# Narrowing one of eight weight groups in a later stage of a fused attention and mixer kernel

## The chip, the cores and the metric

The kernel runs on one core of one Trainium2 chip. The metric is device time in microseconds (us) of one execution, the median of several runs. Engines are named as in the profile: PE is TensorE (matmuls; PEld is its weight load), DVE is VectorE, ACT is ScalarE, POOL is GpSimd, SP is SyncE, whose queue issues all the DMAs spoken of here.

## What is computed

Three blocks follow each other on 8 sequences of 576 tokens with 512 features. The change touches a weight of the third.

```python
# 1 attention in chunks of 64 tokens, 8 heads of 64
# 2 h = relu(x @ w_in); conv over 3 tokens; (h * sigmoid(conv)) @ w_out
# 3
X = fft(fft(x, axis=1), axis=2)
u = x + real(X)
un = (u - mean(u)) / sqrt(var(u) + 1e-6)
out = u + relu(un @ w_ch1) @ w_ch2        # w_ch1 512 x 2048, w_ch2 2048 x 512
```

Weights arrive as 64-bit floats and are narrowed to 32 bits by the kernel itself.

## The kernel before

**Stages.** In the first part the kernel runs attention, block 2 and the Fourier transforms, half a sequence (16 of them) at a time. In the second part it computes relu(un @ w_ch1) in six chunks of tokens and, in each chunk, eight groups g = 0 to 7 of features (`group`, six-matmul products on L855). The third part multiplies by w_ch2 (`second`, L922). Each of the last two products is a block scheme with seven products in place of eight: each group has the products B11, B21, T2, T1, T3, T4 and B22, and their weights are four blocks of w_ch1 and four sums of blocks, T1 to T4.

**Weights of the second part.** For each group of w_ch1, `weight_sums` loads two pieces of 512 KB (`wide`), narrows each with `to_float32` (four DVE instructions, L278, L279, L281 and L282, and one ACT instruction, L280), makes the four sums in `block_sums` (DVE, one on L661 and three on L660), and stores blocks and sums to the DRAM scratch `t_scr` (L668 for the blocks, L669 for the sums). This happens in the first part for all eight groups, one started every 9 steps. For w_ch2 the same work, `weight_sums_late`, runs within chunks 1 to 4 of the second part.

**From the scratch back.** `load_tw(0, g)` brings a group back in two pieces, k = 0 (512 KB: the weights of B11, B21, T2, T1) and k = 1 (384 KB: T3, T4, B22), each into a staging tile `ts`, and splits it into `th` (ACT cast, L265) and `tl` (DVE subtraction, L266). A product multiplies th by sxh, th by sxl and tl by sxh, in this order, so its third matmul needs `tl`. The split tiles of groups 0 to 7 stay for all chunks; chunk 0 is where they are filled. The tiles of groups 2 to 7 lie in a pool `e` that takes the room of pools of the first part, and so wait for the last users of that room.

**The ring of ts.** `ts` has three buffers, used strictly in the order in which the program asks for them: a tile starts when the third tile before it is done with (all writers and readers). `weight_sums_late` takes three tiles of this ring at once: `wide` (also the place of the sums), `x` and `both`.

```python
            ring = plan.rings.setdefault((pool, tag), [])
            self.before = ring[-bufs] if len(ring) >= bufs else None
        wide, x, both = (buf("b", "ts", 3, *shape) for shape in (([128, 512], I64), ([128, 512],), ([128, 1024],)))
```

**What sets the order.** A planner (`Plan.emit`) simulates the engines with a cost for each operation and writes out a fixed order for each engine's queue: of the operations that are ready by its own clock, the one with the lowest priority number goes first. A priority unit is about 1 us in the second part, where group g of chunk 0 has priorities from `start + 7 * g`. On the chip each queue runs in that order and waits at each operation for what it needs.

**Order of ts in chunk 0.** The tiles are asked for in this order: group 0 (two), one for the left operands, group 1 (two), group 2 (two), group 3 (two), and so on to group 7.

Of the kernel before, what the change touches and what calls it, by code (L numbers as in the profile page):

```python
# [8 lines left out]
F32 = mybir.dt.float32  # L9
# [11 lines left out]
FT = 8  # L21
# [15 lines left out]
FG = 8  # L37
# [48 lines left out]
class Plan:  # L86
# [10 lines left out]
    def buf(self, pool, tag, bufs, shape, dtype=F32):  # L97
        return Buf(self, pool, tag, bufs, shape, dtype)

    def op(self, eng, cost, fn, prio, r=(), w=(), after=(), nbytes=0, spare=0):  # L100
        o = Op()
        o.spare = spare
        o.eng, o.cost, o.fn, o.prio, o.nbytes, o.seq = eng, cost, fn, prio, nbytes, len(self.ops)
        o.slots = [b for b in w if b.tag in self.ANY_ORDER and not b.writers]
        deps = {}
        for b in r:
            assert b.writers and not b.closed, b.tag
            for d in b.writers:
                deps[d] = True
        for b in w:  # L110
            assert not b.closed, b.tag
            if not b.writers:
                if b.pool in self.opened:
                    deps[self.opened[b.pool]] = True
                if b.before is not None:
                    for d in b.before.writers + b.before.readers:
                        deps[d] = True
                if b.previous is not None and b.previous not in w:
                    deps.setdefault(b.previous.writers[0], False)
            for d in b.writers + b.readers:  # L120
                deps[d] = True
        for d in after:
            deps[d] = True
        for b in r:
            b.readers.append(o)
        for b in w:
            b.writers.append(o)
        o.held = [b for b in {id(b): b for b in (*r, *w)}.values() if b.tag in self.ANY_ORDER]
        for b in o.held:
            b.left += 1  # L130
        o.deps, o.users = deps, []
        for d in deps:
            d.users.append(o)
        o.left, o.ready, o.end = len(deps), 0.0, None
        self.ops.append(o)
        return o
# [73 lines left out]
def kernel(  # L210
# [44 lines left out]
    def load(dst, src, nbytes, prio, r=(), after=()):  # L255
        return op("SP", 450, lambda: sp.dma_start(out=dst(), in_=src()), prio, r=r, w=[dst], after=after, nbytes=nbytes)

    def vop(n, fn, prio, r, w, fast=False, scalars=0):
        return op("DVE", dve_cost(n, fast, scalars), fn, prio, r=r, w=w)
# [13 lines left out]
    def to_float32(f, x, wide, n, prio, view=lambda t: t):  # L273

        word = lambda t, k: t.rearrange("p (n two) -> p n two", two=2)[:, :, k]
        lo, hi = lambda: word(wide().bitcast(U32), 0), lambda: word(wide().bitcast(U32), 1)
        ff, fb, xb = lambda: view(f()), lambda: view(f()).bitcast(U32), lambda: x().bitcast(U32)
        vop(n, lambda: dve.tensor_scalar(xb(), hi(), 3, 0x3FFFFFF8, op0=ALU.logical_shift_left, op1=ALU.bitwise_and), prio, [wide], [x], fast=True)  # L278
        vop(n, lambda: dve.scalar_tensor_tensor(fb(), in0=hi(), scalar=0xC0000000, in1=xb(), op0=ALU.bitwise_and, op1=ALU.bitwise_or), prio, [wide, x], [f])  # L279
        aop(n, lambda: act.activation(out=x(), in_=word(wide().bitcast(F32), 1), func=ACT.Abs), prio, [wide], [x])  # L280
        vop(n, lambda: dve.scalar_tensor_tensor(fb(), in0=lo(), scalar=29, in1=fb(), op0=ALU.logical_shift_right, op1=ALU.bitwise_or), prio, [wide, f], [f])  # L281
        vop(n, lambda: dve.scalar_tensor_tensor(ff(), in0=x(), scalar=LEAST_NORMAL, in1=ff(), op0=ALU.is_ge, op1=ALU.mult), prio, [x, f], [f])  # L282
# [371 lines left out]
    def block_sums(n, g, a, b, r, ts, tv, prio):  # L654

        lo, hi = slice(0, 256), slice(256, 512)
        b11, b12, b21, b22 = ((a, lo), (b, lo), (a, hi), (b, hi)) if n == 0 else ((a, lo), (a, hi), (b, lo), (b, hi))
        at = lambda x: x[0]()[:, x[1]]
        t = lambda i: tv()[:, 256 * (i - 2):256 * (i - 2) + 256]
        sub = lambda i, x, y: vop(256, lambda: dve.tensor_tensor(t(i), x(), y(), op=ALU.subtract), prio, [*r, ts], [ts])  # L660
        vop(256, lambda: dve.tensor_tensor(t(T1), at(b12), at(b11), op=ALU.subtract), prio, r, [ts])  # L661
        sub(T2, lambda: at(b22), lambda: t(T1))
        sub(T3, lambda: at(b22), lambda: at(b12))
        sub(T4, lambda: at(b21), lambda: t(T2))
        dst = t_scr[n][g]
        parts = [(0, 512, a, slice(0, 512))] if n == 0 else [(0, 256, a, lo), (256, 512, b, lo)]
        for c0, c1, x, xs in [*parts, (1536, 1792, b, hi)]:
            op("SP", 450, lambda c0=c0, c1=c1, x=x, xs=xs: sp.dma_start(out=dst()[:, c0:c1], in_=x()[:, xs]), prio + 0.5, r=r, w=[dst], nbytes=512 * (c1 - c0))  # L668
        op("SP", 450, lambda: sp.dma_start(out=dst()[:, 512:1536], in_=tv()), prio + 0.5, r=[ts], w=[dst], nbytes=524288)  # L669
# [10 lines left out]
        ts = buf("w", "wide", 2, [128, 1024])  # L680
        block_sums(0, g, *fs, fs, ts, ts, prio + 3.5)

    def weight_sums_late(g, srcs, prio):

        wide, x, both = (buf("b", "ts", 3, *shape) for shape in (([128, 512], I64), ([128, 512],), ([128, 1024],)))
        for k, src in enumerate(srcs):
            load(wide, lambda src=src: src, 524288, prio - 8 + 2 * k)
            to_float32(both, x, wide, 512, prio + 2 * k, view=lambda t, k=k: t[:, 512 * k:512 * k + 512])
        a, b = (lambda k=k: both()[:, 512 * k:512 * k + 512] for k in range(2))
        block_sums(1, g, a, b, [both], wide, lambda: wide().bitcast(F32), prio + 4)  # L690

# [8 lines left out]
    def load_tw(n, g, prios):  # L702
        tw[n, g] = []
        for k, (c0, c1) in enumerate(CUTS):
            s = buf("b", "ts", 3, [128, c1 - c0])
            src = t_scr[n][g]
            op("SP", 450, lambda s=s, src=src, c0=c0, c1=c1: sp.dma_start(out=s(), in_=src()[:, c0:c1]), prios[k] - 6, r=[src], w=[s], nbytes=512 * (c1 - c0))
            hl = tuple(buf("b" if g < 2 else "e", f"t{x}{k}{g}", 1, [128, c1 - c0], F32R) for x in "hl")
            tw[n, g].append(hl)
            if (n, g) == (0, 0):  # L710
                whole["t", k] = s
            split(*hl, s, c1 - c0, prios[k], after=() if n or g else last_fold)
# [240 lines left out]
        load_weight(w_in[:, f, :], wi, -2 + f)  # L953
        load_weight(w_out[:, f, :], wo, 0 + f)
    rows = lambda src: [[src[:, f, :] for f in (g, FG + g)] for g in range(FG)]
    later = list(enumerate(rows(w_ch1)))
    for i in range(NH):
        t = i * FT
        if i + 1 < NH:
            for q in range(2):  # L960
                attention(i + 1, q, t - 3.5 + 3 * q)
        for f in range(FT):
            step = m_step(i, f, t + f)
            x_step(i, f, t + f + lag)
            while later and t + f >= FT + 9 * (FG - len(later)):
                weight_sums(*later.pop(0), t + f + 8, [step])
            if t + f == 88:
                stats_first([88 + 2 * n for n in range(2 * HT)])
            if t + f in (103, 111, 119):
                norm_first((t + f - 103) // 8, t + f)  # L970
        if i == 0:
            load_dft(14)
        if i % 2:
            b, t = i // 2, t + FT + lag
            fold(b, t + 1)
            for sine in range(2):
                for m in range(3):
                    d_step(b, m, sine, t + 2.5 + m + 0.5 * sine)
            for m in range(3):
                s_step(b, m, t + 5 + m if b == B - 1 else t + 6 + 2 * m)  # L980
# [17 lines left out]
    start = end + 8  # L998
# [3 lines left out]
    begun = [group(0, 0, end)]  # L1002
    for g in range(1, FG):
        load_tw(0, g, [start + 7 * g - 7, start + 7 * g - 3])
    for c in range(NCH):
        t = start + span * c
        begun = begun if c == 0 else []
        for g in range(len(begun), FG):
            begun.append(group(c, g, t + 7 * g))
            if 1 <= c <= 4 and g in (0, 2):  # L1010
                n = 2 * (c - 1) + g // 2
                weight_sums_late(n, rows(w_ch2)[n], t + 7 * g + 10)
        if c + 1 < NCH:
            prep(c + 1, [t + 7 * g for g in (2, 3, 4, 4, 5, 6)], [begun[g] for g in ((1, 3) if c else (3, 5))])
    t = start + span * NCH
# [125 lines left out]
```

## Time and profile before

| | us |
|---|---|
| median of 3 runs (1356.93 to 1362.35) | 1359.32 |
| the profiled execution | 1358.73 |
| its span, first to last instruction | 1357.0 |
| PE busy in the span | 1322.6 (97%) |
| DVE busy | 1048.2 (77%) |
| ACT busy | 801.2 (59%) |

The page gives busy time per engine over the span. PE's matmuls follow each other at a fixed pace when nothing holds them: 42 matmuls of 384 columns of one group take about 7.3 us. The granted clock is 0.996 of full speed on average.

### The profile page before, as it was taken

Reading aid. Unit: us, or ns where it says so; the run is one execution under the profiler, and the core shown is the slowest. Engines: PE = TensorE matmul, PEld = TensorE weight load, DVE = VectorE, ACT = ScalarE, POOL = GpSimd, SP = SyncE. Lnnn points to the kernel's source line nnn. Section 1 sums busy time; section 2 is a strip of 40 time slices with the busy share of each in tenths; the row PEclk is TensorE's granted clock in tenths of the full one; section 3 lists DMA queues with packets and bytes.
Section 4 is the critical chain, followed back from the end, with each engine's and each line's share of the span. In section 5 each row is a group of like instructions: output and inputs, shape, how many; then the busy total and the mean of one; then the engine's idle time right before and its main releaser. Section 6 shows DMA issues by size and latency. Waiting matters only on the chain.

```text
span 1357.0 us, 29644 instructions
## 1 busy us (share of the span) xinstructions
PE 1322.6 (97%) x11362; PEld 1288.9 (95%) x11362; DVE 1048.2 (77%) x2017; ACT 801.2 (59%) x2181; POOL 73.4 (5%) x190
## 2 busy tenths in 40 slices
PE   5899999999999999998999999999999999999999
PEld 4699999999999999987999999999999999999998
DVE  7999897889977676767777676765598777777773
ACT  6777675868676676646766665656763333333331
POOL 1111020101001110200000000000000000000000
PEclk9999999999999999998999999999999999999999
DMA  8523614232522132135766657669855554554441
GB/s 307 159 84 116 191 58 151 83 123 95 187 87 79 62 116 60 57 128 175 250 189 186 201 163 230 183 194 294 247 160 182 174 173 133 164 171 142 154 140 40
DMA packets 154573, 206.50 MB, mean 152 GB/s; under 512 B 11584, under 2 KB 103360, under 8 KB 154432
## 3 DMA queue, kind: packets, MB, share of 16 engines
q1 hardware_dynamic: 154432, 204.61, 48.1%
q8 instruction: 89, 1.46, 0.4%
q14 instruction: 52, 0.43, 0.1%
HBM read 130.51 MB, written 74.06 MB: 151 GB/s over the span
## 4 chain that ended last, share of the span: by engine, by line
PE 91%; DVE 4%; ACT 2%; issue 1%; DMA 0%; POOL 0%; ACTq 0%; DVEq 0%
PE x L855 21%; PE x L922 15%; PE o L451 14%; PE x L516 14%; PE o L922 11%; PE o L855 4%; PE o L586 3%; PE o L614 2%; PE o L635 1%; PE o L371 1%; PE o L748 1%; PE o L414 1%; PE o L396 1%; DVE cv L468 0%; DMA h_scr<-u 0%
## 5 line engine op out<-in xcount | busy, mean ns | idle before, releaser
L265 ACT CAST sxh<-raw 128x1024 fp32r<-128x1024 f32 (+1 forms) x149 | 146.6, 990 | 186.6 <-PE x L922 83.7
L451 PE MATMUL o<-x,wih 128*128 128x320 f32 (+1 forms) x960 | 198.8, 301 | 1.6 <-DVE x L428 1.0
L266 DVE TENSOR_TENSOR sxl<-raw,sxh 128x1024 fp32r<-128x1024 f32 (+1 forms) x149 | 170.0, 1150 | 35.8 <-ACT sxh L265 35.5
L855 PE MATMUL x<-sxh,th 128*128 128x384 f32 x564 | 190.2, 337 | 2.7 <-ACT th L265 2.1
L855 PE MATMUL x<-sxh,tl 128*128 128x384 f32 x564 | 189.3, 336 | 0.8 <-DVE tl L266 0.8
L855 PE MATMUL x<-sxl,th 128*128 128x384 f32 x564 | 188.8, 335 | 0.0
L922 PE MATMUL x<-th,sxl 128*128 128x256 f32 x576 | 163.3, 283 | 0.5 <-DVE sxl L266 0.5
L922 PE MATMUL x<-th,sxh 128*128 128x256 f32 x576 | 163.3, 283 | 0.2 <-ACT h L832 0.2
L922 PE MATMUL x<-tl,sxh 128*128 128x256 f32 x576 | 163.2, 283 | 0.0
L451 PEld LDWEIGHTS o<-x,wih 128*128 128x128 f32 x960 | 153.3, 188 | 3.9 <-DVE x L428 1.4
L468 DVE SCALAR_TENSOR_TENSOR cv<-h,cw,cv 128x255 f32<-128x255 f32 (+2 forms) x256 | 129.2, 515 | 30.7 <-ACT cv L482 22.8
L823 DVE TENSOR_TENSOR u<-x,u 128x384 f32<-128x384 f32 (+1 forms) x168 | 83.5, 498 | 83.8 <-PE x L922 29.1
L516 PE MATMUL x<-gh,woh 128*128 128x322 f32 (+1 forms) x480 | 145.9, 304 | 0.5 <-ACT gh L265 0.5
L516 PE MATMUL x<-gl,woh 128*128 128x322 f32 (+1 forms) x480 | 142.4, 297 | 0.2
L516 PE MATMUL x<-gh,wol 128*128 128x322 f32 (+1 forms) x480 | 142.5, 297 | 0.0
L451 PE MATMUL o<-x,wil 128*128 128x320 f32 (+1 forms) x480 | 142.1, 296 | 0.0
L922 PE MATMUL o<-th,sxl 128*128 128x256 f32 x432 | 122.4, 283 | 0.0
L922 PE MATMUL o<-tl,sxh 128*128 128x256 f32 x432 | 122.4, 283 | 0.0
L922 PE MATMUL o<-th,sxh 128*128 128x256 f32 x432 | 122.4, 283 | 0.0
L922 PEld LDWEIGHTS x<-th,sxl 128*128 128x128 f32 x576 | 110.7, 192 | 0.7 <-DVE sxl L266 0.7
L922 PEld LDWEIGHTS x<-th,sxh 128*128 128x128 f32 x576 | 110.7, 192 | 0.5 <-ACT h L832 0.5
L922 PEld LDWEIGHTS x<-tl,sxh 128*128 128x128 f32 x576 | 110.7, 192 | 0.0
(273 smaller groups left out, 3217.8 us busy)
## 6 DMA issues: line engine op xcount, KB each, us to landing
raw<-h_scr SPq DMA_DIRECT2D x72, 512.0 KB, 4.4
h_scr<-u SPq DMA_DIRECT2D x96, 192.0 KB, 2.8
u<-u_scr SPq DMA_DIRECT2D x66, 256.0 KB, 4.3
qk<-in_qk_b SPq DMA_DIRECT2D x32, 320.0 KB, 3.5
h_scr<-m SPq DMA_DIRECT2D x48, 192.0 KB, 3.1
h_scr<-h SPq DMA_DIRECT2D x48, 192.0 KB, 2.8
out_y<-u SPq DMA_DIRECT2D x35, 256.0 KB, 2.4
wide<-in_w_ch SPq DMA_DIRECT2D x16, 512.0 KB, 4.3
```

The lines of the kernel that those rows point to most:

```text
L265: aop(n, lambda: act.copy(out=cut(h()), in_=cut(src())), prio, [src], [h], psum, after=after)
L266: vop(n, lambda: dve.tensor_tensor(cut(l()), cut(src()), cut(h()).bitcast(F32), op=ALU.subtract), prio, [src, h], [l])
L371: pe.matmul(s[h]()[half[u], slot, :], t[half[h], 0, ks], t[half[h], 1, ks], start=True, stop=True)
L396: pe.transpose(tps[k // 4]()[:, k % 4, :], flat[:, 128 * k:128 * k + 128], ident)
L451: pe.matmul(acc(), w[:, ws], x, start=k == 0, stop=k == 11)
L468: vop(hi - lo, lambda: dve.scalar_tensor_tensor(cv()[:, lo:hi], in0=h()[:, src:src + hi - lo], scalar=tap(k), in1=cv()[:, lo:hi], op0=ALU. ...
L516: pe.matmul(accs[d](), w[:, dsl], x, start=f == 0 and k == 0, stop=f == FT - 1 and k == 2)
L586: pe.matmul(acc()[:rows, :], x, w, start=n == 0, stop=n == len(todo) - 1)
L614: pe.matmul(accs[sine]()[:rows, :], w, x, start=n == 0, stop=n == len(todo) - 1)
L823: vop(n, lambda: dve.tensor_tensor(cut(x()), acc(), cut(x()), op=ALU.add), prio, [acc, x], [x])
L855: pe.matmul(acc(), a, b, start=first and m == 0, stop=m == 5, skip_group_check=not first)
L922: pe.matmul(acc(), a, b, start=first and m == 0 and gs[0] == 0, stop=gs[-1] == FG - 1 and m == len(todo) - 1, skip_group_check=not first)
```

## The change

The list `later` of the first part loses group 7 of w_ch1, and the remaining seven groups start every 10 steps and not every 9. The narrowing and summing of group 7 is done by `weight_sums_late`, which now takes the number of the weight as `m`. It is asked for in the loop that asks for the `load_tw` of chunk 0, right after that of group 2 and ahead of that of group 3, with priority `start + 10`.

```diff
-    def weight_sums_late(g, srcs, prio):
+    def weight_sums_late(g, srcs, prio, m=1):
...
-        block_sums(1, g, a, b, [both], wide, lambda: wide().bitcast(F32), prio + 4)
+        block_sums(m, g, a, b, [both], wide, lambda: wide().bitcast(F32), prio + 4)
...
-    later = list(enumerate(rows(w_ch1)))
+    later = list(enumerate(rows(w_ch1)[:FG - 1]))
...
-            while later and t + f >= FT + 9 * (FG - len(later)):
+            while later and t + f >= FT + 10 * (FG - 1 - len(later)):
                 weight_sums(*later.pop(0), t + f + 8, [step])
...
     for g in range(1, FG):
         load_tw(0, g, [start + 7 * g - 7, start + 7 * g - 3])
+        if g == 2:
+            weight_sums_late(FG - 1, rows(w_ch1)[FG - 1], start + 10, 0)
```

## Rows read from the trace of the kernel before

**Rows 1.** The page: busy time of each engine, share of the span, instructions.

```profile
PE 1322.6 (97%) x11362; PEld 1288.9 (95%) x11362; DVE 1048.2 (77%) x2017; ACT 801.2 (59%) x2181; POOL 73.4 (5%) x190
```

**Rows 2.** Busy time by stretch: length; PE, PEld, DVE, ACT, POOL busy; clock, DMA share, GB/s.

```profile
108.00:370.00 262.00, 259.88 (x2826) 251.04 (x2826) 230.17 (x548) 186.91 (x692) 32.35 (x88) 1.00 0.39 125
...
646.30:660.00 13.70, 13.70 (x81) 13.70 (x80) 10.84 (x22) 10.61 (x20) 0.00 (x0) 1.00 0.92 304
660.00:680.00 20.00, 20.00 (x125) 19.90 (x124) 16.57 (x36) 14.61 (x32) 0.00 (x0) 1.00 0.73 224
...
760.00:996.00 236.00, 235.85 (x1400) 234.94 (x1399) 157.12 (x297) 146.62 (x305) 0.00 (x0) 1.00 0.71 214
996.00:1357.00 361.00, 357.20 (x2975) 356.93 (x2974) 273.32 (x319) 128.29 (x125) 0.00 (x0) 1.00 0.47 148
```

**Rows 3.** Groups by line, 100 to 370 us: busy us, mean ns of one, idle before.

```profile
L282 DVE SCALAR_TENSOR_TENSOR wf<-wx,wf 128x512 f32<-128x512 f32 x15 | 10.3, 686 | 0.3
L660 DVE TENSOR_TENSOR wide<-wf,wide 128x256 f32<-128x256 f32 x16 | 6.7, 419 | 0.1
L278 DVE TENSOR_SCALAR wx<-wide 128x512 uint32<-128x512 uint32 x15 | 6.3, 419 | 0.1
```

**Rows 4.** SP's queue by time: start, us, DMA issues.

```profile
624.47 2.40 SPq L707 DMA_DIRECT2D ts<-t_scr  x3
630.96 0.57 SPq L707 DMA_DIRECT2D ts<-t_scr  x1
639.78 4.12 SPq L707 DMA_DIRECT2D ts<-t_scr  x3
...
677.30 5.73 SPq L880 DMA_DIRECT2D h_scr<-u  x2
```

**Rows 5.** DVE by time, the splits of groups 1 to 3 and one addition.

```profile
629.24 0.96 DVE L266 TENSOR_TENSOR tl<-ts,th 128x768 fp32r<-128x768 f32 x1 [0.19 <-ACT th L265]
...
638.53 1.23 DVE L266 TENSOR_TENSOR tl<-ts,th 128x1024 fp32r<-128x1024 f32 x1
641.12 0.96 DVE L266 TENSOR_TENSOR tl<-ts,th 128x768 fp32r<-128x768 f32 x1 [1.37 <-DMA u_scr<-u]
642.33 1.23 DVE L266 TENSOR_TENSOR tl<-ts,th 128x1024 fp32r<-128x1024 f32 x1 [0.25 <-ACT th L265]
...
647.03 0.56 DVE L823 TENSOR_TENSOR u<-x,u 128x384 f32<-128x384 f32 x1 [0.19 <-ACT u L831]
```

**Rows 6.** ACT by time, the cast of group 3's first piece.

```profile
641.25 1.04 ACT L265 CAST th<-ts 128x1024 fp32r<-128x1024 f32 x1 [2.14 <-DMA u_scr<-u]
```

**Rows 7.** The chain that ended last, by time: start, us, what.

```profile
641.46 1.72 PE o L855 x6
643.18 4.35 PE x L855 x24
647.53 1.04 PE o L855 x6
```

**Rows 8.** DVE by time: work of the same kind for w_ch2.

```profile
680.70 0.42 DVE L278 TENSOR_SCALAR ts<-ts 128x512 uint32<-128x512 uint32 x1
...
689.58 0.69 DVE L282 SCALAR_TENSOR_TENSOR ts<-ts 128x512 f32<-128x512 f32 x1
690.18 0.42 DVE L661 TENSOR_TENSOR ts<-ts 128x256 f32<-128x256 f32 x1
...
692.02 1.09 DVE L660 TENSOR_TENSOR ts<-ts 128x256 f32<-128x256 f32 x3
...
712.33 0.43 DVE L278 TENSOR_SCALAR ts<-ts 128x512 uint32<-128x512 uint32 x1 [0.17 <-DMA ts<-in_w_ch]
712.79 0.69 DVE L279 SCALAR_TENSOR_TENSOR ts<-ts 128x512 uint32<-128x512 uint32 x1
713.52 0.69 DVE L281 SCALAR_TENSOR_TENSOR ts<-ts 128x512 uint32<-128x512 uint32 x1
714.31 0.69 DVE L282 SCALAR_TENSOR_TENSOR ts<-ts 128x512 f32<-128x512 f32 x1
```

**Rows 9.** SP's queue by time: the two loads for that work.

```profile
708.11 0.62 SPq L256 DMA_DIRECT2D ts<-in_w_ch  x1
...
714.28 0.34 SPq L256 DMA_DIRECT2D ts<-in_w_ch  x1
```

**Rows 10.** L669 (600 to 760 us), L707, L256 (600 to 720), in this order: issue to landing.

```profile
DMA to landing us min/median/max: 2.7/3.2/3.7
...
DMA to landing us min/median/max: 3.0/4.2/5.8
...
DMA to landing us min/median/max: 2.9/4.3/5.4
```

**Rows 11.** PE by time: the pace of matmuls on L855 after a wait.

```profile
638.43 0.45 PE L855 MATMUL x<-sxh,th 128*128 128x384 f32 x1 [2.14 <-ACT th L265]
638.71 0.34 PE L855 MATMUL x<-sxl,th 128*128 128x384 f32 x1
639.81 0.69 PE L855 MATMUL x<-sxh,tl 128*128 128x384 f32 x1 [0.76 <-DVE tl L266]
```

**Rows 12.** Busy time by stretch around that wait, columns as in the second group.

```profile
640.00:642.80 2.80, 2.80 (x9) 2.80 (x10) 1.43 (x2) 1.42 (x2) 0.00 (x0) 0.50 0.65 186
642.80:646.30 3.50, 3.50 (x20) 3.27 (x20) 1.73 (x3) 1.62 (x3) 0.00 (x0) 1.00 0.74 217
```

## The prediction

> **What bounds the kernel now.** I read the busy times first: PE has 1322.6 us of 1357.0, and nothing else comes near [rows 1]. So the question is only where PE stands still, and the stretches say that: between 108 and 370 us, where the weights of w_ch1 are narrowed, PE is idle for 262.00 - 259.88 = 2.1 us, although DVE is busy 230 of 262 us; from 646 us on, through the six chunks, PE has no gap worth a name until the third part starts at 996 us, where 3.8 us are lost [rows 2]. A microsecond of PE idle that is added in chunk 0 therefore reaches the end, for no slack behind it can take it up. After that I followed the ring `ts` through chunk 0: the SP queue for the loads, DVE and ACT for the splits, PE for the first use [rows 4 to 7].
>
> **What is removed from the first part.** Two narrowings of 0.42 + 3 x 0.69 us and four sums of 0.42 us leave DVE, 6.6 us in all [rows 3], with two casts on ACT and five DMAs on SP (two loads, three stores). All of it lay beside matmuls. What PE can gain is its idle time there, 2.1 us at most [rows 2], and of that one group of eight plus the wider spacing should give back a quarter: I take -0.5 us. The order of the queues is written anew by the planner, so the end on the other side is as much: +2 us, the same idle time doubled. The bounds are -2.1 and +2.
>
> **What is added to chunk 0, and where it stands in the ring.** The same 6.6 us of DVE work would fit: DVE has 2.9 us free of 13.7 between 646 and 660 us and 3.4 of 20 after it [rows 2]. The ring is another matter. `wide`, `x` and `both` now stand between the tiles of group 2 and those of group 3. By the rule of three, `wide` takes the place of group 1's second piece, `x` that of group 2's first, `both` that of group 2's second; and group 3's first piece gets the place of `wide`, which is done with only when the sums have been stored from it. Before, group 3's first piece was loaded at 630.96, as soon as the split of group 1's second ended at 630.2, and group 3's second piece at 639.78, as soon as group 2's first was split [rows 4, 5]. That shows that the ring holds on the chip as it is written.
>
> The chain of the changed kernel, step by step:
> - The first load of group 7 can go at about 631, where group 3's load went, and lands long before it is needed.
> - `both` is free when group 2's second piece has been split: 641.12 + 0.96 = 642.1 [rows 5]. This doesn't move; that split waits for a store of the first part.
> - First narrowing, from L279 on, up to the second load, which reuses `wide`: 712.79 to 714.28, 1.5 us [rows 8, 9]. Time 643.6.
> - Second load up to the first instruction on it: 708.11 to 712.33, 4.2 us [rows 8, 9]. Time 647.8.
> - Second narrowing: 712.33 to 714.31 + 0.69, 2.7 us. The four sums: 0.42 + 1.09 = 1.5 us [rows 8]. Time 652.0.
> - One addition of group 2 falls between on DVE, 0.56 us [rows 5]: I take 0.5. Time 652.5.
> - Store of the sums, issue to landing 3.2 us [rows 10]. Time 655.7.
> - Load of group 3's first piece into the place of `wide`, 4.2 us [rows 10]. Time 659.9.
> - Cast 1.04 us and subtraction 1.23 us [rows 5, 6]. Time 662.2. The third matmul of B11 waits for this; its two forerunners take 0.35 us, so group 3 counts as started at 661.8.
>
> Before, PE began group 3 at 643.18 + 18 x 0.173 = 646.3: of the 24 matmuls in that piece of the chain, 18 are T2, T1 and T3 of group 2 and the last six B11 of group 3, and B21 of group 3 follows [rows 7]. Of group 2, T4 and B22 are then left, 12 matmuls of 0.173 us, which can fill 2.1 us. PE has nothing else: chunk 1's operands are loaded only after group 3 has begun. PE stands from 648.4 to 661.8, 13.4 us.
>
> After a wait of 2.1 and another of 0.8 us at 638 to 640, the granted clock of the next stretch was 0.50, that is 1.2 of 2.4 GHz: 9 matmuls took 2.8 us, against 20 in 3.5 us behind it [rows 11, 12]. That costs 2.8 - 9 x 0.173 = 1.2 us. After a longer wait I take the same, and 2.4, twice that, as its upper end; nothing, if PE is held by other waits in those microseconds, is the lower one.
>
> Behind group 3 the ring runs as before: its second piece and group 4's first get the places of `x` and `both`, free before that of `wide`, and their loads go right behind the first. Their splits follow on ACT and DVE within 3 to 4 us of each other, and a group takes PE 7.3 us. So I count no second gap. Group 7's own weights are in the scratch before group 3's are even loaded, so its `load_tw` waits for nothing new.
>
> **The sum.** -0.5 + 13.4 + 1.2 = 14.1 us. The profiled execution took 1358.73 us, 1357.0 of it span, and stands 0.6 us below the median of the runs shown: 1358.7 + 14.1 = 1372.8 us, 1.0% longer.
>
> Short end of the terms: load 2.9, store 2.7 and load 3.0 us in place of 4.2, 3.2 and 4.2 [rows 10], no addition between: 13.4 - 3.5 = 9.9; no clock loss; -2.1: +7.8, 1366.5 us. Long end: load 5.4, store 3.7, load 5.8 [rows 10] add 3.3; the second narrowing stretched, as at 680.70 to 690.27, to 9.6 us by other work between its instructions [rows 8] adds 6.9; clock 2.4; first part +2: 13.4 + 3.3 + 6.9 + 2.4 + 2 = 28.0, 1386.7 us. All ends at once is unlikely, and other DVE work is scarce while PE stands, so I stay near the short sum.
>
> The Trainium skill ("DMA: Bandwidth & Descriptors", section "Anatomy of one DMA — SWDGE (gpsimd) path") fits a transfer that GpSimd issues as 2.0 us plus bytes at 436 GB/s; here SP issues. An estimate by that page is 3.2 us for each 512 KB transfer here; three of them would be 9.6 in place of 11.6 us, and the time 1370.8. The trace's medians stand higher for the loads, with other transfers about, and the sum goes by the trace.
>
> **The rivals.** *Hidden, not slower (7%).* The tiles could come free so early, or the load of group 3 not be held, that the work disappears beside PE. It decides at one point: group 3's first split must end by 648.4 + 0.35, 13.4 us ahead of my chain. For it speaks that the same work hides in chunks 1 to 4 with no PE gap [rows 2]; against it, that no `load_tw` follows it in the ring there, and that three transfers and two narrowings in a row don't fit between 642.1 and 648.4. It would give 1358.7 - 0.5 = 1358.2 us, down to 1356.6.
> The Trainium skill ("DMA: Bandwidth & Descriptors", section "Rules for kernel authors") advises to issue a transfer early and wait late so that its fixed cost overlaps with compute; by this rule the moved transfers would be hidden. The trace bears that out for chunks 1 to 4 only, and its chance here is the 7%.
>
> *Held up further in the queues (8%).* SP issues in order, and an h_scr store that waits for PE held that queue for up to 5.7 us at 677.30 [rows 4]. If one such store stands between the chain's transfers, with its producer itself behind the gap or behind a waiting DVE instruction, each adds 5.7 us: two give 1372.8 + 11.4 = 1384.2 us and more. Against it: the planner works out the same ring and should place these transfers where its own gap lies.
>
> *The first part gives more than its idle time (2%).* That would need DVE's relief to shorten the matmuls' order itself; beyond 2.1 us I see nothing to give, so a time under 1352 is left as a remainder.
>
> **How the numbers follow.** My forecast, the gap in front of group 3, has 83%, and 1372.8 us. About 0.5%, 6.8 us, is what a measurement of this kernel can tell from no change: from 1352.5 to 1366.1. The forecast's own ends, 1366.5 to 1386.7, lie above that; I leave it 0.03 below them, for a short chain with a better first part. The range leaves out the hidden case's lower part and the far end: 1363 to 1384. Faster 0.02; same 0.07 for the hidden case and 0.03 for a short chain, 0.10; slower 0.88.
>
> **What the profile would show.** In the SP queue a load from w_ch1 at about 631 and another near 644, then stores to the scratch at about 652 and the load of group 3 only behind the last of them. PE idle some 13 us, released by `th` or `tl` of group 3, then a stretch at half the clock, then no gap up to 996 + 14. In the first part PE's idle within a microsecond of 2.1. I would be wrong if group 3's load stood ahead of the sums' store, if PE found other work in the gap, or if the groups behind caught up on it.

## The result, and the profile after

| | before | after |
|---|---|---|
| median of 5 runs, us | 1359.32 (1356.93 to 1362.35) | 1372.54 (1368.14 to 1372.76) |
| the profiled execution, us | 1358.73 | 1372.49 |
| its span, us | 1357.0 | 1370.7 |
| mean granted clock | 0.996 | 0.990 |

After over before is 1.0094, interval 1.0079 to 1.0109: slower by 0.9%. The page of after gives the same number of instructions on every engine as before [rows 1]. PE's busy time grew by 3.2 us of the 13.7 us that the span grew; the other 10.5 us are idle.

```profile
PE 1325.8 (97%) x11362; PEld 1292.6 (94%) x11362; DVE 1046.3 (76%) x2017; ACT 805.3 (59%) x2181; POOL 71.9 (5%) x190
```

The stretches of after, with the columns of [rows 2], say where:

```profile
108.00:370.00 262.00, 260.43 (x2816) 252.68 (x2815) 225.71 (x543) 188.11 (x694) 31.85 (x88) 1.00 0.37 121
640.00:680.00 40.00, 28.92 (x147) 27.70 (x147) 24.46 (x46) 20.33 (x38) 0.00 (x0) 0.83 0.68 216
700.00:773.00 73.00, 73.00 (x431) 72.90 (x431) 53.81 (x106) 46.64 (x100) 0.00 (x0) 1.00 0.64 190
773.00:1010.00 237.00, 236.68 (x1406) 235.79 (x1404) 159.77 (x303) 148.44 (x307) 0.00 (x0) 1.00 0.71 214
1010.00:1371.00 361.00, 357.13 (x2974) 356.93 (x2974) 273.06 (x319) 128.00 (x125) 0.00 (x0) 1.00 0.47 148
...
649.50:659.50 10.00, 0.66 (x4) 0.34 (x2) 3.37 (x7) 2.04 (x4) 0.00 (x0) 0.73 0.81 276
659.50:664.30 4.80, 4.26 (x12) 3.76 (x13) 3.32 (x3) 2.49 (x4) 0.00 (x0) 0.50 0.57 166
664.30:670.00 5.70, 5.70 (x34) 5.70 (x34) 2.70 (x5) 3.75 (x7) 0.00 (x0) 1.00 0.92 316
```

In the first part (first line) PE is idle for 1.57 us, before 2.12. The whole loss lies between 640 and 680 us, where PE stands 11.1 of 40 us. From 700 us on PE stands no longer than before: 0.0, 0.3 and 3.9 us. The last three lines open that place: 10 us in which four matmuls run, 4.8 us at granted clock 0.50 (1.2 of 2.4 GHz), and then full speed with no idle time.

PE by time in after (start, us, what, idle time before it and what ended it) gives the waits one by one:

```profile
639.38 0.44 PE L855 MATMUL x<-sxh,th 128*128 128x384 f32 x1 [2.14 <-ACT th L265]
640.64 0.69 PE L855 MATMUL x<-sxh,tl 128*128 128x384 f32 x1 [0.64 <-DVE tl L266]
...
647.80 0.45 PE L855 MATMUL x<-sxh,th 128*128 128x384 f32 x1 [0.57 <-ACT u L831]
...
649.82 0.34 PE L855 MATMUL x<-sxh,tl 128*128 128x384 f32 x1
659.78 0.69 PE L855 MATMUL x<-sxh,th 128*128 128x384 f32 x1 [9.62 <-ACT th L265]
...
661.04 0.69 PE L855 MATMUL x<-sxh,tl 128*128 128x384 f32 x1 [0.25 <-DVE tl L266]
...
664.38 0.33 PE L855 MATMUL x<-sxh,th 128*128 128x384 f32 x1
```

The first two are group 2's, as in [rows 11] (2.14 and 0.76 us there). New are 0.57, 9.62 and 0.25 us, together 10.4. Group 3 then needs 664.38 - 659.78 = 4.60 us for twelve matmuls, of which 0.25 is the wait counted already and 12 x 0.173 = 2.08 its full-speed time: 2.27 us are left, which I put down to the clock (a run below gives it 2.0 of them). Group 2 itself began at 639.38, 0.95 us later than before. The sum is 0.95 + 10.44 + 2.27 = 13.7 us, which is 1370.7 - 1357.0.

SP's queue of after (DMA issues; the lines below the second "..." are the same stretch asked for in narrower windows):

```profile
631.54 0.57 SPq L256 DMA_DIRECT2D ts<-in_w_ch  x1
...
643.42 0.34 SPq L256 DMA_DIRECT2D ts<-in_w_ch  x1
...
651.95 1.06 SPq L668 DMA_DIRECT2D t_scr<-ts  x2
653.77 0.32 SPq L669 DMA_DIRECT2D t_scr<-ts  x1
654.14 8.06 SPq L707 DMA_DIRECT2D ts<-t_scr  x5
...
652.61 0.40 SPq L668 DMA_DIRECT2D t_scr<-ts  x1
...
654.82 0.58 SPq L707 DMA_DIRECT2D ts<-t_scr  x1
...
656.90 0.32 SPq L707 DMA_DIRECT2D ts<-t_scr  x1
```

Two loads of group 7, two stores of its blocks, one of its sums, and 0.05 us behind that store's issue the load of group 3's first piece, at 654.14; before it went at 630.96 [rows 4].

DVE by time in the same stretch:

```profile
639.36 2.09 DVE L266 TENSOR_TENSOR tl<-ts,th 128x1024 fp32r<-128x1024 f32 x2 [0.93 <-ACT th L265]
641.37 0.42 DVE L278 TENSOR_SCALAR ts<-ts 128x512 uint32<-128x512 uint32 x1
...
647.78 0.56 DVE L823 TENSOR_TENSOR u<-x,u 128x384 f32<-128x384 f32 x1 [2.41 <-ACT u L831]
648.26 0.42 DVE L278 TENSOR_SCALAR ts<-ts 128x512 uint32<-128x512 uint32 x1
...
650.20 0.56 DVE L823 TENSOR_TENSOR u<-x,u 128x384 f32<-128x384 f32 x1 [0.80 <-PE x L855]
...
651.47 0.69 DVE L282 SCALAR_TENSOR_TENSOR ts<-ts 128x512 f32<-128x512 f32 x1
...
652.65 1.09 DVE L660 TENSOR_TENSOR ts<-ts 128x256 f32<-128x256 f32 x3
```

And the chain that ended last (start, us, what) goes through this very work:

```profile
652.65 1.11 DVE ts L660 x3
653.77 0.32 SPq L669
654.14 4.45 DMA ts<-t_scr
658.69 1.05 ACT th L265
659.76 1.24 DVE tl L266
```

Sums, issue of their store, load of group 3, its cast, its subtraction, and from 661.04 PE: each link starts within 0.1 us of the end of the one before it.

### The profile page after: what moved, and what is told of

It reads as the page before. It is cut to its first block, busy times and chain, and to the rows that moved or that the text cites. A ratio compares the mean times of both kernels' runs of the same rounds, so it can differ in the third digit from the quotient of the medians.

```text
span 1370.7 us, 29641 instructions
## 1 busy us (share of the span) xinstructions
PE 1325.8 (97%) x11362; PEld 1292.6 (94%) x11362; DVE 1046.3 (76%) x2017; ACT 805.3 (59%) x2181; POOL 71.9 (5%) x190
## 4 chain that ended last, share of the span: by engine, by line
PE 88%; DVE 5%; ACT 3%; issue 1%; DMA 1%; POOL 0%; SPq 0%; ACTq 0%; DVEq 0%; POOLq 0%
PE x L855 21%; PE x L922 15%; PE o L451 13%; PE x L516 13%; PE o L922 11%; PE o L855 4%; PE o L586 3%; PE o L614 2%; PE o L635 1%; PE o L748 1%; PE o L371 1%; PE o L414 1%; PE o L396 1%; DVE cv L468 1%; ACT es L383 1%
## 5 line engine op out<-in xcount | busy, mean ns | idle before, releaser
L855 PE MATMUL x<-sxh,th 128*128 128x384 f32 x564 | 190.6, 338 | 12.9 <-ACT th L265 11.8
L855 PE MATMUL x<-sxh,tl 128*128 128x384 f32 x564 | 189.7, 336 | 0.9 <-DVE tl L266 0.9
L855 PE MATMUL x<-sxl,th 128*128 128x384 f32 x564 | 189.0, 335 | 0.0
L855 PEld LDWEIGHTS x<-sxh,th 128*128 128x128 f32 x564 | 106.5, 189 | 14.4 <-ACT th L265 12.4
```

Source lines behind the costliest of these rows:

```text
L855: pe.matmul(acc(), a, b, start=first and m == 0, stop=m == 5, skip_group_check=not first)
```

## The experiments

All are edits of the changed kernel; runs of the kernel before stood beside each, and the ratios are to those. Theory A is the prediction's: the ring of `ts` and the order of the queues hold group 3's load behind group 7's sums, and PE pays the wait and then the clock. Theory B: what costs is the added work itself, on DVE, ACT and the DMA engines in that stretch. A third question is what the first part gave back.

### The first part alone

```diff
-            src = t_scr[n][g]
+            src = t_scr[n][g if n else min(g, FG - 2)]
...
-        if g == 2:
-            weight_sums_late(FG - 1, rows(w_ch1)[FG - 1], start + 10, 0)
```

> Only the first part's side of the change: seven groups, every 10 steps; group 7 is narrowed nowhere, and its weights are read from group 6's scratch (this leaves out part of the computation). Theory: the first part moves by no more than its idle time, 1357 to 1361 us, and PE reaches 638 us within 1 us of the changed kernel's 639.4, so the 0.95 us of shift seen there come from the new order of the first part. Rival (the first part hides a loss or a gain of several us that the gap covers): under 1355 or over 1363 us.

Measured: 1358.86 us beside 1359.16, ratio 0.9995 (0.9984 to 1.0007). What leaves the first part gives back nothing that can be measured, 2.2 us at the very most by the interval. Its one trace began group 2 at 640.87, 1.5 us from the changed kernel's 639.38 and not within the 1 us expected; why such times scatter stands further down. This kernel doesn't do the moved work at all, so with this first part I take its time as the best that any placement could bring; that is an argument, no run shows it.

### The ring taken away

```diff
-        wide, x, both = (buf("b", "ts", 3, *shape) for shape in (([128, 512], I64), ([128, 512],), ([128, 1024],)))
+        wide, x, both = (buf("b", *(("ts", 3) if m else ("raw", 6)), *shape) for shape in (([128, 512], I64), ([128, 512],), ([128, 1024],)))
```

> As the changed kernel, but the three tiles of group 7's late narrowing come from the ring `raw` (six buffers, idle between the first operands and the preparation of chunk 1) and no longer stand between group 2 and group 3 in the ring `ts`. The work in chunk 0 stays the same. Theory (the ring holds group 3's load behind the chain): the gap of 9.6 us in front of group 3 goes, with the half clock behind it, and what stays is the first part's shift, so 1358 to 1361 us. Rival (the added DVE, ACT and DMA work itself is what delays group 3, wherever its tiles lie): 1368 to 1373 us.

Measured: 1361.96 us beside 1359.16, ratio 1.0016 (1.0004 to 1.0027). The work is the same, in the same stage, but its three tiles come from the ring `raw` and not from `ts`. The wait in front of group 3 is gone, and with it some 80% of the loss: the ring it was, together with the order of SP's queue, which the planner writes by it. The time is 1 us above the range that was expected. What is left shows in two views, PE by time and DVE by time:

```profile
638.59 0.69 PE L855 MATMUL x<-sxh,th 128*128 128x384 f32 x1 [3.42 <-ACT th L265]
...
641.68 0.69 PE L855 MATMUL x<-sxh,tl 128*128 128x384 f32 x1 [2.08 <-DVE tl L266]
```

```profile
639.39 1.09 DVE L660 TENSOR_TENSOR raw<-raw 128x256 f32<-128x256 f32 x3
640.40 3.22 DVE L266 TENSOR_TENSOR tl<-ts,th 128x1024 fp32r<-128x1024 f32 x3
```

The second wait is 2.08 us where [rows 11] has 0.76: the four sums now run early and stand ahead of group 2's subtraction in DVE's queue. That part is theory B's, and it is small. The first wait is longer too, 3.42 against 2.14, but group 2's first matmul comes at nearly the same time as before (638.59 and 638.43): PE only came to the wait earlier.

### The ring taken away, and the work put behind group 2

```diff
-            load(wide, lambda src=src: src, 524288, prio - 8 + 2 * k)
+            load(wide, lambda src=src: src, 524288, prio - 8 + 2 * k, after=after)
...
-            weight_sums_late(FG - 1, rows(w_ch1)[FG - 1], start + 10, 0)
+            weight_sums_late(FG - 1, rows(w_ch1)[FG - 1], start + 26, 0, [plan.ops[-1]])
```

> The tiles in the ring `raw` as in the first experiment, and the load of the first piece of group 7 bound to come behind the split of group 2, with priority start + 26, so that none of the narrowing stands on DVE ahead of the splits of groups 2 and 3. Theory (the 2 us that the ring `raw` left over are DVE's order: the sums at 638.9 to 640.4 stood ahead of group 2's tl): PE waits before group 2 as in the kernel before, 2.1 and 0.8 us, and 1358 to 1360 us. Rival (the left-over is DMA traffic or the first part): 1361 to 1363 us; if group 7 comes too late now, a PE wait before it and more than 1363 us.

Measured: 1368.01 us beside 1358.75, ratio 1.0061 (1.0047 to 1.0075). A miss: group 2's waits are those of before, but the sums, ready at 669.0, are stored at 674.91, behind five `h_scr` stores and a store of the blocks in SP's queue, and group 7, which needs them, waits. SP's queue, then PE:

```profile
674.91 0.59 SPq L669 DMA_DIRECT2D t_scr<-raw  x1
...
680.21 1.06 SPq L707 DMA_DIRECT2D ts<-t_scr  x2
```

```profile
685.92 0.69 PE L855 MATMUL x<-sxh,th 128*128 128x384 f32 x1 [4.63 <-ACT th L265]
```

With only the second load held back (`after=after if k else ()`, and `start + 10` again) the work falls between the two:

> The tiles in the ring `raw`, priority start + 10, and only the load of the second piece bound to come behind the split of group 2: the first narrowing stays in front, the second narrowing and the sums come behind the splits of groups 2 and 3 on DVE. Theory (with the ring out of the way what is left is DVE's order at group 2 and, in the run before with both loads bound, the late store of the sums): PE waits 2.1 and 0.8 us before group 2, no wait over 1 us at groups 3 and 7, 1357.5 to 1360 us, no difference from the kernel before. Rival (the added work costs some 2 us wherever it stands): 1361 to 1363 us; if group 7's sums are still late, a wait before it and 1363 to 1368 us.

Measured: 1362.21 us beside 1357.58, ratio 1.0032 (1.0018 to 1.0045), where 1357.5 to 1360 was expected. This run tells most about theory B: DVE does the second narrowing and the sums from 646.89 to 654.57, in after from 648.26 to 653.74, so the work stands at much the same place, and group 3 doesn't wait. DVE by time, its first line:

```profile
646.89 0.42 DVE L278 TENSOR_SCALAR raw<-raw 128x512 uint32<-128x512 uint32 x1
```

No long wait is left beside group 2's, but short ones, 3.4 us in all from 620 us on above those of before, with a span 3.5 us longer. They are five, of 0.55 to 1.01 us; PE by time, the first and the last two:

```profile
642.26 0.44 PE L855 MATMUL x<-sxh,th 128*128 128x384 f32 x1 [0.62 <-ACT m L831]
...
963.95 0.44 PE L855 MATMUL x<-sxh,th 128*128 128x384 f32 x1 [0.78 <-DVE u L823]
...
965.83 0.44 PE L855 MATMUL x<-sxh,th 128*128 128x384 f32 x1 [0.55 <-ACT h L832]
```

The last two, 1.3 us, lie 300 us behind the moved work, and a wait like the first (0.55 us) stands also in the kernel that doesn't do that work. So what is left here, 4.6 us by the medians, isn't shown to be theory B's: the order of the queues, written anew with each edit, is as likely.

### The place in the ring moved

Asked for after group 1, or after group 5:

```diff
-        if g == 2:
+        if g == 1:
```

> The changed kernel with its request for the three tiles of `ts` moved one group ahead: between groups 1 and 2. Theory (who stands behind the three tiles in the ring waits): the wait moves in front of group 2. The third tile is free when group 1's second piece is split, about 631; with the chain of 12.5 us, 4.4 us of load and 2.3 us of split group 2 would start at about 649 in place of 640, and that wait has its half clock already in the kernel before: 1367 to 1370 us, and no wait before group 3. Rival (group 3's place or the work in that stretch is what costs): the wait stays before group 3 and 1372 us.

```diff
-        if g == 2:
-            weight_sums_late(FG - 1, rows(w_ch1)[FG - 1], start + 10, 0)
+        if g == 5:
+            weight_sums_late(FG - 1, rows(w_ch1)[FG - 1], start + 31, 0)
```

> The changed kernel with its request moved behind group 5's tiles, priority start + 31. Theory: the wait moves in front of group 6. Group 5's second split ends at 659.4 in the kernel before; with 12.7 us of chain, 4.4 of load and 2.3 of split, group 6 starts at about 678.5 in place of 670.7 (668.6 plus 2.1 us of group 5's last products), with about 2 us of half clock: 1368 to 1371 us, up to 1374 if DVE, busier there, stretches the chain. Rival (only groups 2 and 3, beside the end of the first part, are tight): 1359 to 1362 us.

Measured: 1365.24 us (ratio 1.0044, 1.0031 to 1.0058) and 1368.64 us (1.0070, 1.0056 to 1.0084), both beside 1358.75. PE by time, first the one after group 1, then the one after group 5:

```profile
645.54 0.69 PE L855 MATMUL x<-sxh,th 128*128 128x384 f32 x1 [11.44 <-ACT th L265]
```

```profile
674.27 1.64 PE L748 MATMUL o<-ident,u 128*128 128x128 f32 x12 [2.64 <-DVE u L743]
...
680.10 0.69 PE L855 MATMUL x<-sxh,th 128*128 128x384 f32 x1 [4.19 <-ACT th L265]
```

The long wait goes where the request goes: before group 2 in the one, before group 6 in the other, each the group asked for next. That is theory A's mark. Work that only loads DVE would move the wait too, but the kernel with the ring taken away has that load and no such wait. In the first kernel the 11.4 us take the place of group 2's own 2.9 us and of the 10.4 us behind it, and so cost less (1.8 us less than the least expected); in the second 4.2 us are left of it, beside 2.6 us at a step of the normalisation (L743). The rest of its loss is mostly the clock: it is at 0.50 again, and twelve matmuls take from 680.10 to 684.72, 2.3 us too long without the wait of 0.25 for `tl` among them.

### The chain shortened by one load

The second piece of group 7 is not loaded; the first is narrowed twice.

```diff
-            load(wide, lambda src=src: src, 524288, prio - 8 + 2 * k)
+            if m or k == 0:
+                load(wide, lambda src=src: src, 524288, prio - 8 + 2 * k)
```

> As the changed kernel, but the second piece of group 7 is not loaded: both halves are narrowed from the first load (this leaves out part of the computation). Theory (the chain of load, narrowing and sums is what group 3 waits for, step for step): L278 of the second half can start right behind L282 of the first, at 645.4 in place of 648.3, so 3 to 4.5 us less, 1368 to 1370 us, with the PE wait at 5 to 7 us. Rival (another condition sets the wait, such as the store of the sums or DVE's order behind PE): 1372 to 1373 us.

Measured: 1369.10 us beside 1359.16, ratio 1.0069 (1.0053 to 1.0085). That is 3.4 us below the changed kernel's first time, as expected, but only 1.2 below its second (below), and the intervals overlap: the medians decide nothing. In the trace PE waits 8.0 us before group 3, where 5 to 7 were expected. From group 2's first matmul to group 3's third it has 657.07 - 637.01 = 20.06 us, where after has 661.04 - 639.38 = 21.66, so 1.6 us come from the chain, of 3 to 4.5 expected. From the same first matmul the sums end 3.5 us earlier than in after (at 647.88). Where the rest of that gain went stands in SP's queue:

```profile
647.00 0.51 SPq L881 DMA_DIRECT2D h_scr<-u  x1
...
648.97 0.51 SPq L881 DMA_DIRECT2D h_scr<-u  x1
649.58 0.57 SPq L669 DMA_DIRECT2D t_scr<-ts  x1
650.19 8.04 SPq L708 DMA_DIRECT2D ts<-t_scr  x5
```

An `h_scr` store that waits for group 2's results holds the queue up to 647.00; behind it the issues follow each other every 0.6 to 0.7 us, and the sums' store, fifth of them, goes 1.7 us after its data are ready. This is the prediction's second rival in small: behind the chain of tiles lies a queue that binds next.

### PE kept busy through the wait

To price the clock, matmuls whose result nobody reads are put into the gap. 48 of them at a bare priority first:

```diff
+        if c == 0 and g == 3:
+            warm = buf("ps", "o", 4, [128, n])
...
+                for k in range(48):
+                    pe.matmul(warm(), wh[:, 0:128], xh[:, 0:n], start=k == 0, stop=k == 47)
...
+            op("PE", mm_cost(n, passes=48), warm_unit, t + 3.5, r=[tw[0, 2][1][0], sx[0, B22][0]], w=[warm])
```

> As the changed kernel, with 48 matmuls of 384 columns added that PE runs while it waits for group 3; nobody reads their result. They take 48 x 0.173 = 8.3 us of a wait of 9.6 us. Theory (the half clock behind the wait is a cost of its own, 2.3 us: 12 matmuls of group 3 in 4.6 us in place of 2.1): 1370 to 1370.5 us, and the matmuls of group 3 at the full clock from the first. Rival (the wait alone sets the time, the slow matmuls are covered by the wait for tl): 1372 to 1373 us; if the added matmuls delay group 2 or group 3, more.

Measured: 1376.48 us beside 1359.16, ratio 1.0125 (1.0108 to 1.0142). It missed its aim: they ran ahead of group 2's products, at 637.58, and delayed all of it. The sums were ready at 651.96, but their store went at 656.86 and the load of group 3 at 658.47, each behind an `h_scr` store: the second rival again.

Then bound behind group 2's last product (`after=last_b22`):

> The 48 added matmuls again, now bound to come behind group 2's last product, so that they stand in the wait before group 3 and delay nothing ahead of it. They fill 8.3 us of a wait of 9.6 us. Theory (the half clock behind the wait is a cost of its own, 12 matmuls of group 3 in 4.6 us in place of 2.1, of which 0.25 us is the wait for tl): 1.5 to 2.3 us less than the changed kernel, 1370 to 1371 us, and the granted clock stays at full behind the wait. Rival (the clock costs nothing beside the wait): 1372 to 1373 us.

Measured: 1371.02 us beside 1358.75, ratio 1.0088 (1.0074 to 1.0102). Inconclusive: 1.32 and 0.64 us of waiting were left, and the granted clock of the next 3 us was 0.50 all the same. With 60 of them:

> 60 added matmuls behind group 2's last product in place of 48: 60 x 0.173 = 10.4 us, all of the wait before group 3 and some tenths more. In the run with 48 a wait of 1.3 and one of 0.6 us were left, and the granted clock still fell. Theory (the half clock is a cost of its own, which goes once PE has no wait left there): group 3's matmuls 0.17 us apart, and 1369.5 to 1370.5 us (2.3 us less than the changed kernel, some tenths lost to the added matmuls and the wait for tl). Rival (the clock falls there in any case, as it did with 48): 1371 to 1373 us.

Measured: 1370.67 us beside 1357.58, ratio 1.0091 (1.0076 to 1.0107), 0.2 us above the range. Now no wait is left there, and the stretch behind it (columns as above) runs at full speed:

```profile
660.50:664.00 3.50, 3.45 (x21) 3.27 (x20) 2.83 (x4) 2.08 (x4) 0.00 (x0) 1.00 0.65 204
```

Group 3's first twelve matmuls take 662.58 - 660.17 = 2.4 us, in after 4.6. Of these 2.2 us, 0.2 are the shorter idle time before `tl` (0.05 here, 0.25 in after), and 2.0 are the clock's share, shown in the trace. In the medians it isn't: 1370.67 against 1372.54 us, measured at different times. So both were run again side by side, the changed kernel and the one with 60 matmuls:

> The changed kernel itself, timed on the same chip and in the same rounds as the next, because the time of the kernel before moves by 1 to 2 us from one chip to another. Expected: 12.5 to 14 us above the kernel before.

> The changed kernel with the 60 added matmuls in the wait before group 3, beside the changed kernel on one chip. In the trace of the first run group 3's first 12 matmuls took 2.4 us in place of 4.6, at the full clock. Theory (the half clock costs its own 2 us): 1.5 to 2.5 us less than the changed kernel beside it. Rival (those 2 us are taken back by a wait behind it): the same time within 0.7 us.

Measured: 1370.33 us (ratio 1.0077, 1.0060 to 1.0095) and 1368.46 us (1.0069, 1.0054 to 1.0085), beside 1359.60. The changed kernel stands only 10.7 us above the kernel before, where 12.5 to 14 were expected and the first time it was 13.2: a miss. The medians of the two differ by 1.9 us, as the price of the clock would have it, but the intervals overlap: consistent, not resolved. The traces of this pair repeat the price: group 3's first twelve matmuls take 4.6 us in the changed kernel and 2.5 in the other.

The changed kernel's second trace has the same wait, at another place in time:

```profile
656.59 0.69 PE L855 MATMUL x<-sxh,th 128*128 128x384 f32 x1 [9.81 <-ACT th L265]
```

None of the kernels tried is faster than the kernel before.

## Why the prediction was right, and where its sum was not

1372.8 us was predicted for the likeliest case, and 1372.5 measured; the wait stands where it was put, with the releaser that was named. But three of the terms were off, and they cancel: that the sum came out within 0.3 us is luck. The change cost 13.2 us the first time and 10.7 the second, where 14.1 was predicted.

**The first part, -0.5 us.** PE's idle time there fell by 0.55 us, as taken. Yet group 2 began 0.95 us later. That is no effect of the change: the same kernel run again began it at 634.65, 4.7 us earlier, and the first matmul of the second part came between 600.8 and 606.2 us in the fourteen traces, at 603.7 in before, at 604.6 in after and latest of all in the kernel that only drops the work from the first part. What goes with this scatter is the granted clock. A stretch of the second trace of the changed kernel, then one of the three slow ones of after (columns as in [rows 2]):

```profile
25.00:600.00 575.00, 559.85 (x5928) 539.02 (x5927) 474.35 (x1129) 411.36 (x1480) 69.37 (x178) 1.00 0.33 107
```

```profile
428.90:432.10 3.20, 3.20 (x14) 3.20 (x14) 2.11 (x7) 1.08 (x7) 0.00 (x0) 0.50 0.49 182
```

The earliest trace, the second one of the changed kernel, has no stretch at 0.50 before 600 us, the four with one come at 601.9 to 603.7, the four with two at 603.0 to 603.5, after and the three others with three at 604.3 to 605.0, and the latest has four. Without the moved work the time is that of before within 0.16%. The term can't be told from zero, and a single profiled execution carries some us of scatter ahead of the change, which the prediction's sum didn't allow for.

**The gap, 13.4 us.** By the prediction's marks (PE free, and two matmuls ahead of the first that needs `tl`) after has 649.82 + 0.34 = 650.16 and 661.04 - 0.35 = 660.69: 10.5 us. PE came to the wait 1.8 us later than forecast (0.95 from ahead, 0.57 from the wait for a copy on ACT, L831) and left it 1.1 us earlier. The chain, step by step:

| step | predicted, us | after, us | from |
|---|---|---|---|
| group 2's second piece split | at 642.1 | at 641.4 | DVE, 639.36 + 2.09 |
| first narrowing up to the second load | 1.5 | 2.0 | L278 stands in it too; 643.42 |
| second load to first use | 4.2 | 4.8 | 3.5 to landing, then an addition ahead on DVE; 648.26 |
| second narrowing and additions | 3.2 | 3.9 | the second addition waits 0.80 for PE; 652.2 |
| sums | 1.5 | 1.6 | 653.8 |
| **store of the sums** | **3.2** | **0.4** | issue to issue; 654.14 |
| load of group 3 | 4.2 | 4.55 | 658.69 |
| cast and subtraction | 2.3 | 2.35 | 661.04 |

The failed step is the store. "Group 3's first piece gets the place of `wide`, which is done with only when the sums have been stored from it" is not what the chip did: the load left 0.05 us behind the store's issue, 2.7 us before the store landed. The compiled program says the same. In SP's queue (order, line, destination and source, waits):

```
287 L669 DMA t_scr07_119<-ts_10028 128x1024 [waits DMAHW7_49,DMAHW6_49,DVE_49]
288 L707 DMA ts_10176<-t_scr03_115 128x1024
289 L707 DMA ts_10178<-t_scr03_115 128x768 [waits DMAHW5_49,DMAHW4_49,DMAHW0_49]
290 L707 DMA ts_10180<-t_scr04_116 128x1024 [waits DMAHW6_49,DMAHW1_49]
```

Group 3's load carries no wait at all, so its place can't be one that a store had still to read, `wide` or `both`; `x` remains, free when L282 ended at 652.16. The second and third loads do wait for DMAs, and their times fit the other two places: 654.82, when the blocks' second store lands (652.61 and the 2.1 to 2.4 us that L668 takes), and 656.90, right after the sums' store landed (653.77 + 3.1 = 656.87). The addresses in the compiled program settle it (bytes within a partition): `x` lies at 1664, `both` at 5760 and `wide` at 9856, and the three loads, group 3's two and group 4's first, go to 1664, 5760 and 9856 in this order. So the tile took the place that came free first, not the oldest request's; the use strictly in order of request is the planner's rule and not the compiled program's. But the planner had put the load behind the store in the queue, and it is the queue's order, with the sums ahead, that kept group 3's load until 654.14. What that order alone costs was not tried by a kernel of its own: by the times above 654.14 - 652.16, 2.0 us at most.

The 2.8 us saved at the store were mostly eaten by the other steps, which were short by 2.3 in all: the chain was forecast at 20.1 us and took 19.6. More than half of that, 1.3 us at the second load and the second narrowing, is one thing: additions of group 2 that stand ahead of the narrowings on DVE and wait themselves, for ACT (2.41 us at 647.78) and for PE (0.80 at 650.20). Another 0.5 is the first narrowing, which was counted from L279 on although L278 stands in it here, and 0.35 the load. The second load had landed, 3.5 us after its issue, 1.3 us before DVE came to it.

The start of the chain was 0.7 us early although group 2 was 0.95 late, since its second split no longer waited for a `u_scr` store as in [rows 5]. In the compiled order of before that split's subtraction has two DMA waits, in after one. Why the pool handed out its room differently was not followed further.

**The clock, 1.2 us.** The mechanism was right and the size too small: up to 2.27 us, 2.0 by the run with PE kept busy. The prediction took over the nine slow matmuls of group 2 [rows 12]. There the clock fell only within the second wait, behind two matmuls at full pace; stretches of before, columns as in [rows 2]:

```profile
639.00:639.40 0.40, 0.05 (x1) 0.00 (x0) 0.40 (x1) 0.11 (x1) 0.00 (x0) 1.00 0.99 287
639.40:639.80 0.40, 0.00 (x0) 0.00 (x0) 0.35 (x1) 0.00 (x0) 0.00 (x0) 0.51 0.96 288
```

Ten matmuls from 639.81 to 643.01 then took 3.20 us, 1.5 too long. At group 3 the clock had fallen already within the 9.62 us (0.73 on average from 649.5 to 659.5 us), and all twelve matmuls were slow. The upper bound, 2.4, held it. The run with PE kept busy shows that it is the wait that brings the clock down. The price isn't fixed: in the second trace of the changed kernel, 18 matmuls at group 2 took 4.39 us against 3.14 in the first, and the like at group 3 3.72 against 3.12.

**Transfers.** The Trainium skill ("DMA: Bandwidth & Descriptors", section "Anatomy of one DMA — SWDGE (gpsimd) path") fits transfers that GpSimd issues; the estimate by it, 3.2 us for 512 KB, stood beside the sum. Here SP issues: the second load of `wide` landed after 3.5 us and the sums' store after 3.1, near that fit, and the five loads from 654 to 662 us after 3.2 to 5.0 us (median 4.4), the longer ones well above it.

**No second gap** behind group 3 held: 73.00 of 73.00 us busy from 700 us on.

**The rivals.** *Hidden* fell at the point that was named: group 3's first split ended at 661.0 and not by 648.8. *Held up further in the queues* did not come true here, but it is real: it took back some half of what the shortened chain gained, and held sums and load when PE's order was disturbed. *More than its idle time from the first part* fell with the kernel that does only that.

## What to carry to other kernels

Work that fits an engine's free time can still be dear by the staging tiles it takes: before moving it, write down which request comes next in that ring and in the issuing queue, and follow that one to the bound engine. Then ask what the place it comes from gives back, in a run that leaves the work out; here that was nothing that could be measured, so there was little for any placement to win. A total that comes out right proves no term: read each step's end from the trace before trusting the sum the next time.

## What the runs showed that was not expected

- Waits of 1.32 and 0.64 us, with matmuls ahead and between, were followed by a granted clock of 0.50 over the next 3 us, and twelve matmuls took 1.8 us too long (659.56 to 664.07, without the 0.64); with no wait at all it stayed at 1.00. Short waits can cost nearly as much in clock as in idle time: the 2.14 and 0.76 us at group 2 [rows 11] are followed by 2.8 us at 0.50 [rows 12] in the kernel before too.
- Traces of one kernel differ by several us ahead of the change: group 2 began at 639.38 in one and at 634.65 in the other, with the number of stretches at granted clock 0.50 before it. Intervals from one matmul to another compare better than times since the start, but not exactly either: from group 2's first matmul to group 3's third it is 21.66 us in the one and 657.85 - 634.65 = 23.20 in the other, a difference as large as the 1.6 us read from the kernel with one load.
- A DMA issue that waits holds everything behind it on SP: the sums' store went 1.7 us after its data were ready in the kernel with one load, and 5.9 us in the one with the work behind group 2.
